# Strip one's first product by sets, three of them at two levels, in an attention and MLP kernel

## The chip, the cores and the metric

The kernel runs on one core of a Trainium2 chip, as one launch. Its time is the device time of one execution in microseconds (us). The engines of the core work side by side: TensorE (PE) multiplies matrices, VectorE (DVE) and GpSimd (POOL) do elementwise work, ScalarE (ACT) copies and applies functions, and SyncE (SP) issues the transfers between DRAM and the on-chip memory (SBUF). Products come out in banks of a second memory, PSUM, which DVE and ACT read.

## The reference

Linear attention with a normalisation, then an MLP with a squared ReLU, all in float32. q, k and v have the shape (8, 8, 576, 64), w_in is 512 x 2048 and w_out 2048 x 512.

```
kv = einsum('bhsd,bhse->bhde', k, v)
out = einsum('bhsd,bhde->bhse', q, kv)
rms = sqrt(mean(out * out, axis=-1, keepdims=True) + 1e-06)
x = (out / rms * g_norm).transpose(0, 2, 1, 3).reshape(4608, 512)
r = maximum(x @ w_in, 0.0)
result = (r * r) @ w_out
```

## The kernel before

The 4608 tokens are cut into nine strips of 512, a strip into four tiles of 128. Each strip has a first product (x times w_in, then ReLU and square) and a second product (times w_out). PE is saved work by Strassen's scheme in Winograd's form: a product of 2 x 2 blocks is done as seven products of sums of the blocks, and sums of these seven give the four quarters of the result. At one level a product has seven sets; at two levels each set is itself done as seven small products.

- Strip 0's first product is done plainly, its second at one level.
- Strip 1 (`DEEP` = 1) has its first product at one level (`up`, L889) and its second at two (`down_deep`). `up` goes through four groups g of the columns of w_in, and in each through the seven sets p of `ORDER`. Each of the 28 steps is eight matmul instructions of 128 x 256 in the trace. The banks are called A, B and C; `combine` (L845) lets ACT copy the banks of sets 1, 6 and 5 into snapshots (L849), DVE adds a later bank to a snapshot (L902) and does ReLU and square in one instruction (L903), and ACT does both for the last quarter (L907, L908).
- Strips 2 and on (`DEEP_UP` = 2) have both products at two levels. Their first product runs over 55 slots (`up_slot`): the set number n of `UP_SETS` = (1, 6, 7, 5, 2, 3, 4) has its small products (`up_small`) in slots 7n, 7n+2, up to 7n+12. Small products come out in banks A, B and C too: j = 1, 6, 5 are copied or added to snapshots (ACT L1300 or DVE L1295), the others added to a snapshot on DVE (L1295) into `gt`, the quarters of the result. For four sets ReLU and square on ACT (L1233, L1234) are due some slots later. `add_s1` lets POOL add quarter 22 to quarter 12, piece by piece; strip 1 does this on DVE in one instruction of 2048 elements per partition (L1149).
- The operands of the small products: `leaf_x` makes sums of x on POOL, `deep_sums_in` makes sums of blocks of w_in on POOL (seven times three instructions, L1189 and L289) during strip 1 and stores them to DRAM (`w_in_deep`, L1196), from where they are streamed for each strip; `deep_differences_in` replaces a block of w_in by a difference, on POOL, seven times, in strip 2.
- The second product streams two blocks of weights for each of its seven sets (`w_blk`, from `w_out` or `w_deep`, issued by `stream`). Its operands, sums g_s of the quarters, are made on DVE (L1038, L289); `small_products` L1066 multiplies.

The attention of later batches is cut into slices (`transposed_query` L384 on DVE, `key_value` L432 on PE, `query_means` L468 on PE, a normalisation on DVE L498 to L563) which `attend` places between the steps of a strip. A tile of x has to be turned for the first product. Batch one's last tile (n = 8, the first of strip 2's) does it in `features` with four PE transposes (L636) and a copy on ACT (L637). All later tiles go `squares_x` (a DVE transpose of small squares, L643), `send_x` (a store of 256 KB to DRAM, L652) and `fetch_x` (four fetches of 64 KB, L659).

All transfers around the change are issued by SP, in program order. At most eight are on the way: an issue waits for the landing of an older one, and for whoever writes its source or still reads its target. `clock[0]` counts planned microseconds; `tiles_due` and `keys_due` hold transfers with a due time, `drip` issues the rest in between. Blocks of weights and the w_in sums share six buffers (tag `w_blk` of `stream_pool`), the sums of x and g_s eight (`sum_pool`), and from strip 1 on the products have five banks (`fpsum`).

Of the kernel before, what the change touches and what calls it, by code (L numbers as in the profile page):

```python
# [10 lines left out]
FP32 = mybir.dt.float32  # L11
# [9 lines left out]
def kernel(  # L21
# [628 lines left out]
    def send_x(n):  # L650
        d = sent[n] = dram.tile([P, 4, NP, SQ], FP32, name="x_d", tag="x_d", bufs=2 * NT)
        nc.sync.dma_start(out=d, in_=squared.pop(n))  # L652
        tiles_due.append((clock[0] + {9: 30, 10: 36, 11: 24}.get(n, 6), fetch_x, (n,)))

# [51 lines left out]
    slices += [(query_means, (last,)), (K, (2, 0, 1)), (T, (2, 0)), (roots_normalized, (last,)), (T, (2, 1))]  # L706
    slices += [(T, (2, 2)), (T, (2, 3)), (features, (last[0],)), (K, (2, 2, 3))]
    pair_ends = []
# [179 lines left out]

    def up(s, g, p):  # L889
        open_bank(p)  # L890
        rhs = {
            1: halves(s, 0, 0), 2: halves(s, 1, 0), 3: halves(s, 1, 1),
            4: xc[s][3], 5: xc[s][0], 6: xc[s][1], 7: xc[s][2],
        }[p]
        for i in range(2):
            product(p, i, lambda kc: w_in[:, kc, g, A_IN[p], ts(i, P)], lambda kc: rhs[:, :, kc, :], KH)
        dest = quarters(s, g)

        def relu_squared(q):
            def f(b, a):  # L900
                o = dest[q]
                nc.vector.tensor_tensor(out=o, in0=b, in1=a, op=ALU.add)  # L902
                nc.vector.scalar_tensor_tensor(out=o, in0=o, scalar=0.0, in1=o, op0=ALU.max, op1=ALU.mult)  # L903
            return f

        def last(b):
            nc.scalar.activation(dest[21], b, AF.Relu)  # L907
            nc.scalar.activation(dest[21], dest[21], AF.Square)  # L908

        combine(p, relu_squared(11), relu_squared(12), last, relu_squared(22))  # L910

# [190 lines left out]
    def down_deep(s, k, i):  # L1102
        p = DEEP_ORDER[k]
        if k == i == 0:
            stream()
        if s == N_STRIP - 1 and k == 6 and i == 1:
# [19 lines left out]
            return  # L1126
        if k == 0 and s >= DEEP_UP:
            if i == 0:
                return
            for j in (7, 5, 6, 3):  # L1130
                small_products(s, p, (j,))
            stream(2)
            deque(leaf_next[1], 0)
            for slot in sorted(relus):
                relu_squares(slot)
            for slot in sorted(first_s):
                add_s1(s, slot)
            return
# [8 lines left out]
        if i == 1:  # L1147
            if k == 0:
                nc.vector.tensor_tensor(out=q12, in0=q12, in1=q22, op=ALU.add)  # L1149
            if k == 3:  # L1150
                minus(nc.vector, q22, q22, q11)
            if k == 4:
                minus(nc.vector, q21, q21, q11)
            if k == 6:
                deque(together(s, p), 0)
            return
# [22 lines left out]
    w_half = lambda b, kc, f: w_in[:, kc, 2 * f : 2 * f + 2, b]  # L1179

    def deep_sums_in(b):

        if b == 0:
            t = [sum_pool.tile([P, FQ // 2, P], FP32, name=f"w_i{i}", tag="sum") for i in range(3)]
        else:
            whole = stream_pool.tile([P, 4, FQ // 2, P], FP32, name="w_i", tag="w_blk")
            t = [whole[:, i] for i in range(3)]
        s1, s2, s4 = (x.rearrange("p f e -> p (f e)").rearrange("p (g e) -> p g e", g=2) for x in t)
        nc.gpsimd.tensor_tensor(out=s1, in0=w_half(b, 0, 1), in1=w_half(b, 1, 1), op=ALU.add)  # L1189
# [51 lines left out]
    def up_slot(s, slot):  # L1241

        for n, p in enumerate(UP_SETS):
            i, odd = divmod(slot - 7 * n, 2)
            if not odd and 0 <= i < 7:
                up_small(s, n, p, ORDER[i], slot)
# [3 lines left out]
        if at == 0 and 0 < n < 6:  # L1250
            leaf_x(s, n + 1)
        if s == DEEP_UP and at == 0 and n < 7:
            deep_differences_in(A_IN[UP_SETS[n]])
# [79 lines left out]
    for s in range(N_STRIP):  # L1333
# [11 lines left out]
        else:  # L1345
            steps = [(1, up, (s, g, p)) for g in range(NG) for p in ORDER]
        n_up = len(steps)
# [11 lines left out]
        for i, (w, fn, a) in enumerate(steps):  # L1359
# [33 lines left out]
            if s:  # L1393
                clock[0] += 3.2 if i >= n_up else 2.2 if s == DEEP else 1.2
                soon = tiles_due and tiles_due[0][2][0] // NT == s + 1
# [4 lines left out]
                elif not due(keys_due) and not (soon and due(tiles_due)):  # L1400
                    least = 2.1 if s == DEEP else 4.5 if i < n_up else 3.3
                    quiet = n_up * 2 // 3 < i < n_up + 3 or s == DEEP and i > n_up + 9
                    quiet = quiet or s == DEEP and i < n_up and drips and drips[0][0] == load_q_rest
# [3 lines left out]
                if s == DEEP:  # L1407
                    attend(begun + (goal - begun) * min(i + 1, 25) // 25)
                elif i < n_up:
                    attend_between(i, begun, goal, *(2, 34) if s == DEEP_UP else (0, 27), 38)  # L1410
                if s == DEEP and i in (3, 4, 7, 9):
                    if i == 3:
                        last_sums = store_deep_sums(*deep_due.popleft())
                    next(last_sums, None)
                if s == DEEP and i == n_up - 3:
                    leaf_sums(s, 4)
                if s == 1 and i in range(2, 23, 3):
                    deep_sums_in((1, 6, 5, 4, 0, 2, 3)[i // 3])
                if s == 1 and i in (17, 20, 21, 23):
                    stream()  # L1420
# [59 lines left out]
```

## Time and profile before

| | |
|---|---|
| median of 7 runs | 887.17 us (886.42 to 889.76) |
| profiled execution | 886.42 us, a span of 884.6 us in the trace |
| strip 1's first product | 138.6 to 195.4 us of the span |
| strip 1's second product | 195.4 to about 237 us |
| strip 2's first product, with the first set of its second | about 237 to 295 us |
| granted clock of PE | 1.00 in all of these |

Two rows of its transfers with large blocks are `w_blk` from `w_deep`, 1024 KB and 7.1 us from issue to landing (median of 56), and `w_blk` from `w_in_deep`, 768 KB and 5.5 us (of 49).

How to read the profile: times are us from the start of the span. "busy" is the time in which an engine executed something. A group row gives the line, the engine, the operation, the output and inputs, the shape and the count, then the busy time and the mean duration in ns, and then the idle time of the engine just before it with who ended it. A timeline row begins with start and duration. Matmuls overlap their neighbours a little, so the distance of two starts is what one costs. SPq is the queue of issues on SP.

### The profile page before, as it was taken

To read this page: it belongs to the slowest core of one execution; us is meant where nothing else is said; L and a number is where in the kernel's file an instruction comes from. 1 tells how busy PE (TensorE), PEld (TensorE's weight loads), DVE (VectorE), ACT (ScalarE), POOL (GpSimd) and SP (SyncE) were. 2 spreads that over 40 slices of the span, in tenths; PEclk is the share of its full clock that TensorE was granted. 3 is DMA by queue.
4 is the path that set the end of the run, shared out by engine and by line. 5 is a ranking of instruction groups with operands and counts; after the bars stand their busy time and mean duration, and the time that the engine had idled before them with its cause. 6 is when DMAs were issued, how large, how long until landed. Compare 5 with 4: busy or idle time off the path is not lost.

```text
span 884.6 us, 20899 instructions
## 1 busy us (share of the span) xinstructions
PE 875.8 (99%) x8296; PEld 821.5 (93%) x8296; DVE 721.6 (82%) x1239; ACT 352.4 (40%) x805; POOL 307.9 (35%) x316
## 2 busy tenths in 40 slices
PE   8999999999999999999999999999999999999998
PEld 7445888889999999999999999999999999999998
DVE  4999998879778985798778966897888778866887
ACT  4898242320049203740365034902491147102710
POOL 0000005610549133731474045604570447045700
PEclk9999999999999999999999999999999999999999
DMA  9998998999979997889678978897668665884483
GB/s 316 312 315 249 296 380 240 270 349 336 310 197 262 328 330 221 223 323 316 209 216 296 321 226 237 294 335 228 207 218 302 255 211 184 291 295 163 175 314 108
DMA packets 170257, 235.73 MB, mean 266 GB/s; under 512 B 79536, under 2 KB 134576, under 8 KB 161840
## 3 DMA queue, kind: packets, MB, share of 16 engines
q1 hardware_dynamic: 169856, 234.33, 80.8%
q8 instruction: 65, 1.06, 0.5%
q14 instruction: 32, 0.26, 0.1%
q10 hardware_dynamic: 304, 0.07, 0.0%
HBM read 197.66 MB, written 36.70 MB: 265 GB/s over the span
## 4 chain that ended last, share of the span: by engine, by line
PE 94%; ACT 2%; DMA 1%; DVE 1%; SPq 0%; issue 0%; DVEq 0%
PE ps_B L1066 22%; PE ps_A L1283 19%; PE ps_A L1066 17%; PE ps_B L1283 9%; PE ps_A L839 6%; PE ps_C L1283 5%; PE ps_B L839 3%; PE kv_ps L432 2%; PE ps_A L880 2%; PE x_ps L468 2%; PE ps_C L839 2%; PE ps_C L880 2%; PE ps_B L880 1%; DMA w_blk<-w_deep 1%; DMA q<-in_q_dram 1%; PE ps_A L617 1%
## 5 line engine op out<-in xcount | busy, mean ns | idle before, releaser
L1066 PE MATMUL ps_B<-w_blk,g_s 128*128 128x128 f32 x1008 | 123.9, 275 | 0.0
L1066 PEld LDWEIGHTS ps_B<-w_blk,g_s 128*128 128x128 f32 x1008 | 118.1, 192 | 0.1
L1283 PE MATMUL ps_A<-x_l,w_in 128*128 128x128 f32 x784 | 103.8, 275 | 0.3 <-ACT snap L1300 0.3
L289 POOL TENSOR_TENSOR x_l<-xT 128x256 f32<-128x256 f32 x21 | 15.7, 749 | 237.4 <-PE ps_A L1066 188.5
L1283 PEld LDWEIGHTS ps_A<-x_l,w_in 128*128 128x128 f32 x784 | 95.4, 192 | 0.6 <-ACT snap L1300 0.5
L1066 PE MATMUL ps_B<-w_blk,gt 128*128 128x128 f32 x752 | 95.4, 275 | 0.4 <-DMA w_blk<-w_deep 0.4
L1066 PE MATMUL ps_A<-w_blk,g_s 128*128 128x128 f32 x768 | 93.6, 275 | 0.0
L1066 PEld LDWEIGHTS ps_B<-w_blk,gt 128*128 128x128 f32 x752 | 89.6, 192 | 0.7 <-PE ps_B L1283 0.6
L1066 PEld LDWEIGHTS ps_A<-w_blk,g_s 128*128 128x128 f32 x768 | 89.6, 192 | 0.0
L1295 POOL TENSOR_TENSOR snap<-snap,gt 128x512 f32<-128x512 f32 x35 | 45.9, 1311 | 118.7 <-ACT snap L1300 104.4
L1300 ACT COPY snap<-ps_A 128x512 f32<-128x512 f32 x63 | 37.0, 587 | 109.6 <-PE ps_A L1283 100.9
L1233 ACT ACTIVATE gt<-gt 128x512 f32<-128x512 f32 x112 | 70.1, 626 | 12.8 <-DVE gt L1295 12.7
L1066 PE MATMUL ps_A<-w_blk,gt 128*128 128x128 f32 x576 | 72.2, 275 | 0.0
L1234 ACT ACTIVATE gt<-gt 128x512 f32<-128x512 f32 x112 | 70.6, 631 | 3.6
L1066 PEld LDWEIGHTS ps_A<-w_blk,gt 128*128 128x128 f32 x576 | 68.2, 192 | 0.0
L1082 ACT COPY o_sb<-ps_A 128x128 f32<-128x128 f32 x24 | 6.4, 266 | 148.4 <-PE ps_A L1066 142.4
L1081 DVE TENSOR_TENSOR o_sb<-o_sb,ps_B 128x256 f32<-128x256 f32 (+1 forms) x123 | 47.4, 385 | 17.2 <-ACT o_sb L1082 12.3
L289 DVE TENSOR_TENSOR gt<-gt 128x2048 f32<-128x2048 f32 (+1 forms) x29 | 59.7, 2063 | 0.0
L1295 POOL TENSOR_TENSOR gt<-gt,snap 128x512 f32<-128x512 f32 x42 | 52.4, 1275 | 17.6 <-DVE snap L1295 17.4
L1283 PE MATMUL ps_B<-x_l,w_blk 128*128 128x128 f32 x392 | 52.1, 276 | 0.0
L1283 PE MATMUL ps_A<-x_l,w_blk 128*128 128x128 f32 x392 | 51.9, 275 | 0.0
L1081 DVE TENSOR_TENSOR o_sb<-o_sb,ps_A 128x256 f32<-128x256 f32 (+1 forms) x96 | 37.1, 387 | 15.1 <-ACT o_sb L1082 10.6
(193 smaller groups left out, 1819.6 us busy)
## 6 DMA issues: line engine op xcount, KB each, us to landing
w_blk<-w_deep SPq DMA_DIRECT2D x56, 1024.0 KB, 7.1
w_blk<-w_out SPq DMA_DIRECT2D x56, 768.0 KB, 6.2
w_blk<-w_in_deep SPq DMA_DIRECT2D x49, 768.0 KB, 5.5
raw<-in_moe_w_in_dram SPq DMA_DIRECT2D x16, 512.0 KB, 6.9
raw<-in_moe_w_out_dram SPq DMA_DIRECT2D x16, 512.0 KB, 5.9
k<-in_k_dram SPq DMA_DIRECT2D x29, 256.0 KB, 4.5
v<-in_v_dram SPq DMA_DIRECT2D x29, 256.0 KB, 5.2
x_d<-x_q SPq DMA_DIRECT2D x27, 256.0 KB, 5.1
```

The lines of the kernel that those rows point to most:

```text
L289: eng.tensor_tensor(out=out, in0=a, in1=b, op=ALU.subtract)
L432: nc.tensor.matmul(ps[ts(h, D), i], lhsT=a, rhs=w, start=i == 0 and c == 0, stop=c == C, skip_group_check=True)
L468: nc.tensor.matmul(ps[half, r, i, ts(p, D)], lhsT=q[row, half], rhs=kvd[b, p][row, row], start=True, stop=True)
L839: nc.tensor.matmul(bank[BANK[p]][:, i, :], lhsT=lhsT(k), rhs=rhs(k), start=p in (1, 5, 2) and i == 0 and k == 0, stop=k == n - 1, skip_gro ...
L880: nc.tensor.matmul(ps, lhsT=w_in[:, kc % KH, g, kc // KH * 2 + fh, ts(i, P)], rhs=xt[0][:, :, kc, :], start=kc == 0, stop=kc == NP - 1,)
L1066: nc.tensor.matmul(chain[c][x][:, i, :], lhsT=a[:, f, :], rhs=w[:, f, :], start=x not in opened[c] and f == 0, stop=f == FQ // 2 - 1, skip ...
L1081: add = lambda out, a, b: nc.vector.tensor_tensor(out=out, in0=a, in1=b, op=ALU.add)
L1233: nc.scalar.activation(o, o, AF.Relu)
L1234: nc.scalar.activation(o, o, AF.Square)
L1283: nc.tensor.matmul(ps[:, i, :], lhsT=w, rhs=rhs, start=j in (1, 2, 5) and i == 0, stop=True, skip_group_check=True)
L1295: add = lambda eng, out, a, b: eng.tensor_tensor(out=out, in0=a, in1=b, op=ALU.add)
L1300: nc.scalar.copy(t, ps)
```

## The change

Strip 1's first product goes set by set instead of group by group. Sets 1, 6, 7 and 5 stay at one level (`up_set`): 16 steps, each with a bank of its own, which ACT copies into the result (set 1) or DVE adds to a quarter (sets 6, 7 and 5; set 5's bank is added to two). Sets 2, 3 and 4 go through `up_slot` as in later strips, slots 28 to 54, with 21 small products. The first of these slots stand between the last steps of set 5. The second product's first set has its small products partly in slots 49, 51 and 53, as later strips have, and POOL's `add_s1` does what L1149 did.

For that POOL makes the w_in sums of sets 2, 3 and 4 first, and these stay in SBUF for strip 1 besides going to DRAM; the sums of x for these sets and three of the seven differences of w_in move from strip 2 into strip 1.

Batch one's last tile is transposed on DVE, stored and fetched like the later ones. Streams, drips and slices of attention are placed by new step numbers.

```diff
--- before.py
+++ after.py
@@ -650,7 +650,7 @@
     def send_x(n):
         d = sent[n] = dram.tile([P, 4, NP, SQ], FP32, name="x_d", tag="x_d", bufs=2 * NT)
         nc.sync.dma_start(out=d, in_=squared.pop(n))
-        tiles_due.append((clock[0] + {9: 30, 10: 36, 11: 24}.get(n, 6), fetch_x, (n,)))
+        tiles_due.append((clock[0] + {8: 50, 9: 30, 10: 36, 11: 24}.get(n, 6), fetch_x, (n,)))
 
     def fetch_x(n):
         s, i = divmod(n, NT)
@@ -704,7 +704,7 @@
     ready[1] = len(slices)
     T, K, last = transposed_query, key_value, query_pairs(1)[2]
     slices += [(query_means, (last,)), (K, (2, 0, 1)), (T, (2, 0)), (roots_normalized, (last,)), (T, (2, 1))]
-    slices += [(T, (2, 2)), (T, (2, 3)), (features, (last[0],)), (K, (2, 2, 3))]
+    slices += [(T, (2, 2)), (squares_x, last), (T, (2, 3)), (send_x, last), (K, (2, 2, 3))]
     pair_ends = []
     for b in range(2, B):
         pairs = query_pairs(b)
@@ -886,28 +886,26 @@
         for th in range(2):
             nc.scalar.activation(dest[(11, 12, 21, 22)[2 * fh + th]][:, i, :], ps[:, ts(th, TH)], AF.Square)
 
-    def up(s, g, p):
-        open_bank(p)
-        rhs = {
-            1: halves(s, 0, 0), 2: halves(s, 1, 0), 3: halves(s, 1, 1),
-            4: xc[s][3], 5: xc[s][0], 6: xc[s][1], 7: xc[s][2],
-        }[p]
+    def up_set(s, g, p):
+        rhs = {1: lambda: halves(s, 0, 0), 5: lambda: xc[s][0], 6: lambda: xc[s][1], 7: lambda: xc[s][2]}[p]()
+        ps = fpsum.tile([P, 2, TH], FP32, name="ps_D", tag="f")
         for i in range(2):
-            product(p, i, lambda kc: w_in[:, kc, g, A_IN[p], ts(i, P)], lambda kc: rhs[:, :, kc, :], KH)
+            for kc in range(KH):
+                nc.tensor.matmul(
+                    ps[:, i, :], lhsT=w_in[:, kc, g, A_IN[p], ts(i, P)], rhs=rhs[:, :, kc, :],
+                    start=i == kc == 0, stop=kc == KH - 1, skip_group_check=True,
+                )
         dest = quarters(s, g)
-
-        def relu_squared(q):
-            def f(b, a):
-                o = dest[q]
-                nc.vector.tensor_tensor(out=o, in0=b, in1=a, op=ALU.add)
-                nc.vector.scalar_tensor_tensor(out=o, in0=o, scalar=0.0, in1=o, op0=ALU.max, op1=ALU.mult)
-            return f
-
-        def last(b):
-            nc.scalar.activation(dest[21], b, AF.Relu)
-            nc.scalar.activation(dest[21], dest[21], AF.Square)
-
-        combine(p, relu_squared(11), relu_squared(12), last, relu_squared(22))
+        add = lambda q, a: nc.vector.tensor_tensor(out=dest[q], in0=ps, in1=dest[a], op=ALU.add)
+        if p == 1:
+            nc.scalar.copy(dest[11], ps)
+        elif p == 5:
+            add(22, 21)
+            add(12, 12)
+            nc.scalar.activation(dest[22], dest[22], AF.Relu)
+            nc.scalar.activation(dest[22], dest[22], AF.Square)
+        else:
+            add(*{6: (12, 11), 7: (21, 12)}[p])
 
     for p, t in zip((1, 2, 5), w_first):
         w_blk[0, p] = t.rearrange("p f (h e) -> p h f e", h=2)
@@ -1101,7 +1099,7 @@
 
     def down_deep(s, k, i):
         p = DEEP_ORDER[k]
-        if k == i == 0:
+        if k == i == 0 and s >= DEEP_UP:
             stream()
         if s == N_STRIP - 1 and k == 6 and i == 1:
 
@@ -1124,7 +1122,7 @@
                         eng = nc.scalar if j == 3 else nc.sync
                         send_quarter(s, 0, 1, o, *divmod(to.start, 2), eng)
             return
-        if k == 0 and s >= DEEP_UP:
+        if k == 0:
             if i == 0:
                 return
             for j in (7, 5, 6, 3):
@@ -1145,8 +1143,6 @@
             stream()
         q11, q12, q21, q22 = (gq[s, q] for q in (11, 12, 21, 22))
         if i == 1:
-            if k == 0:
-                nc.vector.tensor_tensor(out=q12, in0=q12, in1=q22, op=ALU.add)
             if k == 3:
                 minus(nc.vector, q22, q22, q11)
             if k == 4:
@@ -1178,6 +1174,8 @@
 
     w_half = lambda b, kc, f: w_in[:, kc, 2 * f : 2 * f + 2, b]
 
+    IN_SET = {b: p for p, b in A_IN.items()}
+
     def deep_sums_in(b):
 
         if b == 0:
@@ -1185,6 +1183,8 @@
         else:
             whole = stream_pool.tile([P, 4, FQ // 2, P], FP32, name="w_i", tag="w_blk")
             t = [whole[:, i] for i in range(3)]
+            if UP_SETS[4:].count(IN_SET[b]):
+                w_blk["in", DEEP, IN_SET[b]] = whole.rearrange("p n f e -> p n (f e)")
         s1, s2, s4 = (x.rearrange("p f e -> p (f e)").rearrange("p (g e) -> p g e", g=2) for x in t)
         nc.gpsimd.tensor_tensor(out=s1, in0=w_half(b, 0, 1), in1=w_half(b, 1, 1), op=ALU.add)
         minus(nc.gpsimd, s2, s1, w_half(b, 0, 0))
@@ -1242,14 +1242,14 @@
 
         for n, p in enumerate(UP_SETS):
             i, odd = divmod(slot - 7 * n, 2)
-            if not odd and 0 <= i < 7:
+            if not odd and 0 <= i < 7 and (s > DEEP or n >= 4):
                 up_small(s, n, p, ORDER[i], slot)
         if slot in SUM_AT:
             sum_x(s, SUM_AT[slot])
         n, at = divmod(slot, 7)
         if at == 0 and 0 < n < 6:
             leaf_x(s, n + 1)
-        if s == DEEP_UP and at == 0 and n < 7:
+        if at == 0 and n < 7 and (s == DEEP_UP and n < 4 or s == DEEP and n > 4):
             deep_differences_in(A_IN[UP_SETS[n]])
         relu_squares(slot)
         add_s1(s, slot)
@@ -1343,7 +1343,14 @@
         elif s == 0:
             steps = [(2, up_first, (g, fh, i)) for g in range(NG) for fh in range(2) for i in range(2)]
         else:
-            steps = [(1, up, (s, g, p)) for g in range(NG) for p in ORDER]
+            x_sums[s, 4] = xc[s][3]
+            by_set = [(2, up_set, (s, g, p)) for p in UP_SETS[:4] for g in range(NG)]
+            small_ones = [(1, up_slot, (s, slot)) for slot in range(28, 55)]
+            steps = by_set[:13] + small_ones[:1] + by_set[13:14] + small_ones[1:3] + by_set[14:15]
+            steps += small_ones[3:5] + by_set[15:] + small_ones[5:]
+            small_steps = {28, 30, 32, 34, *range(35, 55)}
+            work = [2 if fn == up_set else a[1] in small_steps for _, fn, a in steps]
+            passed = [sum(work[: i + 1]) / 2 for i in range(len(steps))]
         n_up = len(steps)
         if s < DEEP:
 
@@ -1391,7 +1398,7 @@
                 convert(3 + i)
             done += w
             if s:
-                clock[0] += 3.2 if i >= n_up else 2.2 if s == DEEP else 1.2
+                clock[0] += 3.2 if i >= n_up else 1.1 * work[i] if s == DEEP else 1.2
                 soon = tiles_due and tiles_due[0][2][0] // NT == s + 1
                 if i == n_up + 10:
                     while tiles_due and tiles_due[0][2][0] // NT == s + 1:
@@ -1399,24 +1406,27 @@
                         f(*a)
                 elif not due(keys_due) and not (soon and due(tiles_due)):
                     least = 2.1 if s == DEEP else 4.5 if i < n_up else 3.3
-                    quiet = n_up * 2 // 3 < i < n_up + 3 or s == DEEP and i > n_up + 9
+                    quiet = s > DEEP and n_up * 2 // 3 < i < n_up + 3
+                    quiet = quiet or s == DEEP and (i > n_up + 9 or i < n_up + 3 and passed[min(i, n_up - 1)] > 19)
                     quiet = quiet or s == DEEP and i < n_up and drips and drips[0][0] == load_q_rest
                     if not quiet and clock[0] >= dripped[0] + least:
                         dripped[0] = clock[0]
                         drip(True)
                 if s == DEEP:
-                    attend(begun + (goal - begun) * min(i + 1, 25) // 25)
+                    attend(begun + (goal - begun) * min(int(passed[min(i, n_up - 1)]), 23) // 23)
                 elif i < n_up:
                     attend_between(i, begun, goal, *(2, 34) if s == DEEP_UP else (0, 27), 38)
                 if s == DEEP and i in (3, 4, 7, 9):
                     if i == 3:
                         last_sums = store_deep_sums(*deep_due.popleft())
                     next(last_sums, None)
-                if s == DEEP and i == n_up - 3:
-                    leaf_sums(s, 4)
-                if s == 1 and i in range(2, 23, 3):
-                    deep_sums_in((1, 6, 5, 4, 0, 2, 3)[i // 3])
-                if s == 1 and i in (17, 20, 21, 23):
+                if s == DEEP and i in (1, 3, 5, 7, 10, 12, 15):
+                    deep_sums_in({1: 6, 3: 2, 5: 3, 7: 1, 10: 5, 12: 4, 15: 0}[i])
+                if s == DEEP and i == 8:
+                    leaf_x(s, 4)
+                if s == DEEP and i == 9:
+                    deep_differences_in(2)
+                if s == DEEP and i in (18, 22):
                     stream()
                 continue
             if i == n_up:
```

## The prediction

> **What bounds the kernel now.** I read the page's busy times and its chain of waits first:
>
> ```profile
> PE 875.8 (99%) x8296; PEld 821.5 (93%) x8296; DVE 721.6 (82%) x1239; ACT 352.4 (40%) x805; POOL 307.9 (35%) x316
> ...
> PE 94%; ACT 2%; DMA 1%; DVE 1%; SPq 0%; issue 0%; DVEq 0%
> ```
>
> TensorE (PE) is the whole story: 875.8 of 884.6 us busy, 94% of the chain. Its work has to shrink, or something has to make it wait. An average can hide a stage, so next I took the busy times of four stretches: strip 1's first product (138.2 to 195.4), its second product, and strip 2's first product in two parts.
>
> ```profile
> core 0: us, PE busy (x) PEld busy (x) DVE busy (x) ACT busy (x) POOL busy (x), PEclk, DMA share, GB/s
> ...
> 138.20:195.40 57.20, 57.20 (x512) 49.37 (x512) 45.96 (x71) 16.54 (x34) 29.60 (x21) 1.00 0.94 281
> 195.40:237.00 41.60, 41.60 (x375) 41.60 (x374) 39.27 (x59) 2.82 (x8) 7.08 (x7) 1.00 0.98 323
> 237.00:287.00 50.00, 50.00 (x607) 49.25 (x606) 36.44 (x63) 30.77 (x79) 36.06 (x38) 1.00 0.87 242
> 287.00:333.00 46.00, 45.28 (x403) 44.93 (x402) 39.75 (x61) 7.35 (x16) 12.51 (x13) 1.00 0.94 331
> ```
>
> PE never pauses before 287. But VectorE (DVE) has only 11.24 us to spare in strip 1's first product, and the DMA share is 0.94 to 0.98. So a gain on PE is limited by DVE and DMA, not by ScalarE (ACT) or GpSimd (POOL). The clock is 1.00, so no gain or loss comes from there.
>
> **The change part by part.** *Products.* The timeline of PE, start, length, line and shape, once in strip 1 and once in strip 2:
>
> ```profile
> 191.80 1.89 PE L839 MATMUL ps_B<-xT,w_in 128*128 128x256 f32 x8
> 193.53 1.89 PE L839 MATMUL ps_A<-x_t,w_in 128*128 128x256 f32 x8
> ...
> 276.71 1.06 PE L1283 MATMUL ps_A<-x_l,w_blk 128*128 128x128 f32 x8
> 277.61 1.06 PE L1283 MATMUL ps_A<-x_l,w_in 128*128 128x128 f32 x8
> ```
>
> Starts, not lengths, give the price, because neighbours overlap: a large product costs 193.53-191.80 = 1.73 us (1.726 over several), a small one 277.61-276.71 = 0.90 (0.893 over several). Before, strip 1 has 28 large products: 48.33 us. After, it has 16 large ones (four sets, four groups) and 21 small ones (three sets): 27.62 + 18.75 = 46.37. That is -1.96 us. The small products of the second product's first set only move into the first product: same number, same price.
>
> *The last tile of batch one.* Its four PE transposes go; four such took 0.44 us on PE. -0.44 us. In their place DVE does one transpose (0.70, the same form that later tiles use), and SP issues one store of 256 KB and four fetches of 64 KB. 512 KB at the 302 GB/s moved between 210 and 236 us is 1.7 us of DMA time, on no engine's path as long as the weight blocks keep their lead; the third rival prices the case where they don't. The store waits for its DVE transpose and holds the loads queued behind it on SP.
>
> So PE alone gains 2.40 us. All else can only take from that, except in strip 2.
>
> *DVE.* Added: 16 adds of a bank (L899 of the new file) and 18 adds of the small products at 0.68, one transpose at 0.70: 23.8 us. Removed: 12 adds L902 at 0.68, 12 relu-and-multiply L903 at the 1.01 of the row below, and L1149 of 2.29 us: 22.6 us. The total hardly moves (+1.2 us), but its place does: the early adds wait for nobody, while from slot 32 on PE needs each sum to get a bank back.
>
> ```profile
> L903 DVE SCALAR_TENSOR_TENSOR gt<-gt 128x512 f32<-128x512 f32 x12 | 12.1, 1010 | 0.4
> ...
> 161.46 0.71 DVE L384 STREAM_TRANSPOSE qT<-q 128x512 f32<-128x512 f32 x1 [2.38 <-DMA q<-in_q_dram]
> ```
>
> *First place, slot 32.* The second row is a transpose that waits for its q: DVE lay idle 2.38 us, until 161.46. In the new order the sums of the fifth large set stand behind that same wait. If q lands when it did, DVE is free at 162.1 and then has about 11 us to do before the sum that slot 32 waits for: two sums of weights (0.65 and up to 1.3), six bank adds (0.62 apart: 3.7), two reductions (1.27), the mean, the root and its Newton steps (1.2), two scalings (1.29), one more transpose (0.70) and the sum itself (0.68): 173.0. Counting PE's products and attention work from 138.6 by the prices above, PE gets there at 171.7. Between 0 (q lands 1.3 us sooner) and 1.3 us; I take 0.4, because the wait before is that of one late transfer and the queue ahead of it changes.
>
> *Second place, slots 35 to 54.* These are the very slots of strip 2, so strip 2 shows what they cost PE:
>
> ```profile
> PE ps_B L1066 <- DMA w_blk<-w_deep: 0.4, 1, 0.4
> PE ps_B L1283 <- DVE snap L1295: 0.3, 1, 0.3
> ...
> 194.30 0.69 DVE L289 TENSOR_TENSOR g_s<-g_s,gt 128x512 f32<-128x512 f32 x1
> ...
> 280.20 1.11 DVE L1038 TENSOR_TENSOR g_s<-gt 128x512 f32<-128x512 f32 x1
> 282.43 1.80 DVE L289 TENSOR_TENSOR g_s<-g_s,gt 128x512 f32<-128x512 f32 x1
> ...
> 282.41 1.27 POOL L289 TENSOR_TENSOR w_in<-w_in 128x512 f32<-128x512 f32 x1
> ```
>
> The first two rows are all that PE waited for between 195 and 300 us: 0.3 us for a DVE sum in these slots. The rows below tell why it is so near: a sum g_s of two SBUF tiles takes 0.69 us with POOL idle (194.30) and 1.11 to 1.80 with POOL at work (282.43, beside POOL's 282.41). Before, strip 1 makes its g_s with POOL idle; after, POOL adds there and differences w_in there as well. Strip 1 also carries about 2 us of the second batch's attention in these slots, which strip 2 doesn't. By counts DVE has 16.1 to 18.5 us to do for 16.1 us of PE, so the cost is 0 to 2.4 us; I take the row of the same slots, 0.3.
>
> The Trainium skill, "SBUF — State Buffer", "Who interferes with whom", calls the port pair that VectorE and GpSimd share an exclusive lock: with two SBUF inputs VectorE is blocked for the whole GpSimd instruction. It speaks for the new bank adds, which read one SBUF input, and against the g_s sums here: blocked for a whole 1.27 each, five of them would take 9.8 us, and slots 35 to 54 would cost some 6 us; the 1.11 to 1.20 of most rows says that a part of the block is usually over when DVE comes.
>
> *Strip 2* loses three of POOL's differences of w_in, two of them (277.70 and 282.41) amid the g_s above. The 0.3 us wait should go with them: -0.3 us (0 to -0.3). The wait of 0.4 us for a weight block stays.
>
> *POOL* gets three differences, three sums of snaps and four additions at 1.27 and three operand sums at 1.74 into 138 to 195 us: 17.9 us on top of 29.60, of 55. It hides in the idle 25 us. Its additions end last, and DVE's next reader of them comes only in the third set of the second product.
>
> *ACT* gets some 40 instructions and loses 21, about 0.6 us each, on 16.54 of 57.2: hidden.
>
> **Sum.** -1.96 - 0.44 + 0.4 + 0.3 - 0.3 = -2.0 us. The profiled run took 886.42 (a span of 884.6 and 1.8 around it) and would take 884.4. The median of the runs is 887.17, 0.75 above it; from there it is 885.2 us.
>
> **The rivals.** *DVE takes the saving.* Both places at their upper ends, 1.3 + 2.4, and no relief in strip 2: -2.40 + 3.7 = +1.3, 888.5; at the middle of both, 0.65 + 1.2, -0.55, 886.6. For it: DVE is at 80% of the stage and moved to its end, with 2 us of attention. Against it: strip 2 does the same slots for 0.3. As the likely time of this case I take 887.2: no change.
>
> *Late transfers decide, slower.* The place is the run of weight blocks that strip 1's second product reads. SP issued the two blocks of its sixth product late:
>
> ```profile
> 224.23 0.45 SPq L937 DMA_DIRECT2D w_blk<-w_out x1
> ...
> 226.28 0.38 SPq L943 DMA_DIRECT2D w_blk<-w_deep x1
> ...
> w_blk<-w_deep SPq DMA_DIRECT2D x3, 1024.0 KB, 7.4
> ```
>
> The first lands, at the 7.4 us of the neighbouring blocks, at 231.6, and PE's sixth product starts at 232.77: a lead of 1.1 us. The new order ends the strip 2 us sooner, puts a fourth tile's fetches (four, about 0.39 us of SP each: 1.6) and 1.7 us of DMA time before these blocks, and POOL's sums, stored in another order, can hold SP while PE or DVE is late. It decides once more than about 1.1 us of delay reach these blocks. 2 + 1.6 + 1.7 - 1.1 = 4.2 us of waiting against 2.4 gained: +1.8, 889.0, and more if the first blocks (issued from 180 on) slip too. Against it: the extra fetches may be issued before the queue is tight, and an earlier free buffer lets blocks start sooner.
>
> *Nothing held up at all*: both places 0, -2.7, 884.5; inside the forecast's own range.
>
> **Numbers.** A measurement of this kernel tells about 0.2%, 1.8 us, from no change. Forecast, faster: 0.46; DVE takes the saving, no change: 0.27; late transfers or a worse DVE, slower: 0.27. The time is the forecast's, 885.2; its own range 884.3 to 886.2. The whole range takes in no hold-up at the low end, with the median's 0.5 us of scatter (884.0), and at the other end most of the slow case, 889.6. Faster 0.46, same 0.27, slower 0.27.
>
> **What would show it.** Strip 1's first product should end at about 193 to 194 us by PE's own work (moved small products left out), with the second product of it free of waits. PE's waits should list a DVE sum around slot 32 and one or two in the slots after 35, under 1 us together; over 2 us there is the first rival. Waits of L1064 for w_blk over 0.5 us between 190 and 237 are the second. g_s in strip 1 should take 1.1 to 1.2 us instead of 0.69; strip 2's 0.3 us wait should be gone. The prediction is wrong if q lands later than 161.5, if POOL's sums make PE wait, or if strip 2 waits where it didn't.

## The result, and the profile after

The changed kernel is slower: 890.88 us (median of 19 runs, 889.09 to 897.9) against 887.49 (46 runs of the kernel before); the ratio is 1.0039, with a 95% interval of 1.0029 to 1.0050, some 3.4 us. The forecast was 885.2. The profiled execution took 890.58 us, a span of 888.8, which is 4.2 us longer than the span before.

The page's busy times and chain, as shown of the kernel before:

```profile
PE 876.0 (99%) x8364; PEld 823.1 (93%) x8364; DVE 720.6 (81%) x1249; ACT 362.8 (41%) x823; POOL 320.8 (36%) x332
...
PE 80%; DVE 9%; DMA 7%; ACT 2%; issue 1%; SPq 1%; DVEq 0%; ACTq 0%
```

PE is no less busy than before (875.8), although its work shrank, and its share of the chain fell from 94% to 80%: DVE and DMA now hold it up. PE's own waits between 100 and 300 us say where (who waited, for whom, us in total, times, the longest):

```profile
PE kv_ps L432 <- DMA v<-in_v_dram: 2.5, 1, 2.5
PE ps_B L1283 <- DVE snap L1295: 1.4, 2, 1.3
PE ps_A L1283 <- DVE snap L1295: 0.3, 1, 0.3
PE ps_A L839 <- DVE o_sb L1009: 0.3, 1, 0.3
PE ps_B L1064 <- DMA w_blk<-w_deep: 0.2, 1, 0.2
```

And PE's timeline around the first two (start, length, line, what; in brackets the idle time before and who ended it):

```profile
175.21 1.05 PE L1283 MATMUL ps_B<-x_l,w_i 128*128 128x128 f32 x8
176.20 0.69 PE L432 MATMUL kv_ps<-v,k 128*64 128x64 f32 x16
179.42 1.12 PE L432 MATMUL kv_ps<-v,k 128*64 128x64 f32 x16 [2.54 <-DMA v<-in_v_dram]
...
181.03 1.80 PE L468 MATMUL x_ps<-kv_all,qT 64*64 64x64 f32 x60
...
198.22 1.06 PE L1064 MATMUL ps_B<-w_blk,gt 128*128 128x128 f32 x8
200.54 1.16 PE L1283 MATMUL ps_B<-x_t,w_i 128*128 128x128 f32 x8 [1.26 <-DVE snap L1295]
```

Three things are to be read here. The key-value product stops halfway for a v that is not there, 2.54 us. The matmuls after it are slow: 16 of them take 1.12 us, where the same 16 took 0.69 just before, and 60 products of x take 1.80 instead of 1.10. And at slot 52 PE waits 1.26 us for a sum on DVE. The window from 176 to 184 shows the slow ones in the granted clock, 0.79:

```profile
core 0: us, PE busy (x) PEld busy (x) DVE busy (x) ACT busy (x) POOL busy (x), PEclk, DMA share, GB/s
176.00:184.00 8.00, 5.38 (x118) 4.92 (x117) 2.38 (x5) 5.63 (x11) 7.33 (x8) 0.79 1.08 303
197.00:207.00 10.00, 8.74 (x78) 8.55 (x77) 9.06 (x12) 6.72 (x12) 5.69 (x4) 1.00 0.82 316
```

The balance of strip 1, from its first product to the first large group of its second product's second set: 138.45 to 201.50 before, 63.05 us; 138.92 to 206.89 after, 67.97. If PE's work there shrank by the 2.4 that the prediction priced, some 7.3 us were lost. By distances of starts: 2.7 for v, 1.5 for slow matmuls, 1.4 at slot 52, 1.0 in slots 45 to 47, 0.5 at slot 32, the rest in pieces of 0.1. Strip 1 began 0.5 us later, and some 1 us came back after it.

Why v is late is seen on SP's timeline. After, and then before:

```profile
170.15 0.68 SPq L132 DMA_DIRECT2D k<-in_k_dram  x1
170.88 0.63 SPq L132 DMA_DIRECT2D v<-in_v_dram  x1
171.60 0.50 SPq L1196 DMA_DIRECT2D w_in_deep<-w_i  x1
172.19 0.38 SPq L132 DMA_DIRECT2D k<-in_k_dram  x1
172.63 1.36 SPq L132 DMA_DIRECT2D v<-in_v_dram  x1
```

```profile
166.77 0.42 SPq L132 DMA_DIRECT2D k<-in_k_dram  x1
167.24 0.50 SPq L132 DMA_DIRECT2D v<-in_v_dram  x1
167.83 0.42 SPq L132 DMA_DIRECT2D k<-in_k_dram  x1
168.30 0.47 SPq L132 DMA_DIRECT2D v<-in_v_dram  x1
```

The second v goes out at 172.63 instead of 168.30. Counted on SP's timelines from 138 us on, 1.9 MB more than before stand ahead of it: two more stores of w_in sums (768 KB each, one of them between the two pairs), one more store of a turned tile (256 KB) and two more pieces of q (64 KB each). At the 296 GB/s moved from 160 to 176 us that would be some 6.6 us (an estimate). This v also took 6.7 us to land instead of 5.4, so it was there about 5.6 us later than before. Over the whole span the changed kernel moves only 0.55 MB more (236.28 against 235.73): most of the 1.9 MB is the same transfers in another order.

### The profile page after: what moved, and what is told of

The parts are those of the page before. It is cut to its first block, busy times and chain, and to the rows that moved or that the text cites. A ratio compares the mean times of both kernels' runs of the same rounds, so it can differ in the third digit from the quotient of the medians.

```text
span 888.8 us, 21096 instructions
## 1 busy us (share of the span) xinstructions
PE 876.0 (99%) x8364; PEld 823.1 (93%) x8364; DVE 720.6 (81%) x1249; ACT 362.8 (41%) x823; POOL 320.8 (36%) x332
## 2 busy tenths in 40 slices
DMA packets 170979, 236.28 MB, mean 266 GB/s; under 512 B 79616, under 2 KB 135168, under 8 KB 162560
## 4 chain that ended last, share of the span: by engine, by line
PE 80%; DVE 9%; DMA 7%; ACT 2%; issue 1%; SPq 1%; DVEq 0%; ACTq 0%
PE ps_B L1064 22%; PE ps_A L1283 19%; PE ps_A L1064 17%; PE ps_B L1283 9%; PE ps_C L1283 5%; PE ps_D L894 3%; DMA v<-in_v_dram 2%; PE kv_ps L432 2%; PE x_ps L468 2%; DVE w_c L269 2%; DVE w_t L289 1%; DMA q<-in_q_dram 1%; DMA w_deep<-w_t 1%; DVE wt L289 1%; DMA raw<-in_moe_w_in_dram 1%
## 5 line engine op out<-in xcount | busy, mean ns | idle before, releaser
L1283 PE MATMUL ps_A<-x_l,w_in 128*128 128x128 f32 x832 | 110.2, 275 | 0.3 <-ACT snap L1300 0.3
L1283 PEld LDWEIGHTS ps_A<-x_l,w_in 128*128 128x128 f32 x832 | 101.2, 192 | 0.8 <-ACT snap L1300 0.5
L1295 POOL TENSOR_TENSOR snap<-snap,gt 128x512 f32<-128x512 f32 x38 | 49.7, 1309 | 130.2 <-ACT snap L1300 112.1
L1233 ACT ACTIVATE gt<-gt 128x512 f32<-128x512 f32 x124 | 77.6, 626 | 17.6 <-DVE gt L1295 17.4
L1234 ACT ACTIVATE gt<-gt 128x512 f32<-128x512 f32 x124 | 78.2, 631 | 3.9
L1173 POOL TENSOR_TENSOR gt<-gt 128x512 f32<-128x512 f32 x32 | 52.8, 1670 | 0.0
```

Source lines behind the costliest of these rows:

```text
L1173: nc.gpsimd.tensor_tensor(out=a, in0=a, in1=b, op=ALU.add)
L1233: nc.scalar.activation(o, o, AF.Relu)
L1234: nc.scalar.activation(o, o, AF.Square)
L1283: nc.tensor.matmul(ps[:, i, :], lhsT=w, rhs=rhs, start=j in (1, 2, 5) and i == 0, stop=True, skip_group_check=True)
L1295: add = lambda eng, out, a, b: eng.tensor_tensor(out=out, in0=a, in1=b, op=ALU.add)
```

## The experiments

Each was timed beside runs of the kernel before on the same chip; "before" is their median.

### Is it the place of a few transfers in the queue?

The stores of the w_deep parts and one store of w_in sums behind the loads of k and v:

```diff
             for _ in deep_sums(parts, w):
                 if p == 4:
                     yield
+            if p == 4:
+                yield
             for i, t in enumerate(parts):
                 nc.sync.dma_start(out=w_deep[B_OUT[p], :, i], in_=t)
...
-                if s == DEEP and i in (3, 4, 7, 9):
+                if s == DEEP and i in (3, 4, 7, 9, 14):
```

> The changed kernel, but in strip 1 the four stores of w_deep parts and one store of w_in sums are issued behind the loads of k, v and their rests instead of ahead of and between them. Theory A (the late v is the loss): these loads go out some 3 us sooner, PE's pause of 2.54 us for v goes and with it the slow matmuls after it, about 1.4 us; 890.9 - 3.9 = about 887, the waits for DVE sums staying at about 1.3 us at slot 52. Rival B (DVE is the bound and the pause only hides it): the wait for v goes, but the waits for DVE sums grow by as much; within 1 us of the changed kernel, 890 to 891.

Measured: 894.46 us, before 886.97; 1.0078 (1.0059 to 1.0096). The wait for v did go, and yet it is slower than the changed kernel. PE's timeline and two windows of it:

```profile
184.88 1.06 PE L1288 MATMUL ps_A<-x_t,w_in 128*128 128x128 f32 x8
191.99 2.04 PE L1288 MATMUL ps_A<-x_l,w_in 128*128 128x128 f32 x8 [6.05 <-ACT snap L1305]
193.83 1.91 PE L1288 MATMUL ps_C<-x_t,w_in 128*128 128x128 f32 x8
```

```profile
184.00:192.00 8.00, 1.95 (x19) 1.78 (x17) 3.78 (x7) 0.85 (x3) 6.62 (x8) 0.92 0.60 193
192.00:197.00 5.00, 5.00 (x23) 5.00 (x24) 4.90 (x11) 3.46 (x7) 4.15 (x3) 0.50 1.02 402
```

The wait is put down to a copy on ACT, but ACT had 0.85 of 8 us to do. POOL is what stood: busy 0.68 us from 176 to 184, where it had 7.33, very likely because its next sums share their eight buffers with the w_deep parts, whose stores were now issued from 176.3 to 179.3 (the trace itself names PE as what released it); it caught up in the window shown (6.62). Neither theory foresaw that. The second window shows something else: after 6 us of pause the clock is 0.50 and a small product takes 1.91 us instead of 1.06.

One q behind k and v, and nothing else moved:

```diff
+                    quiet = quiet or s == DEEP and 8 <= i < 13
                     if not quiet and clock[0] >= dripped[0] + least:
```

> The changed kernel, but the four loads of one q, which DVE needs only at 185.5 us, are issued behind the loads of k and v that PE needs at 176, not ahead of them; the stores stay where they are. Theory A (the queue ahead of v is the loss): k and v go out about 2 to 3 us sooner, the wait for v is under 0.5 us, the granted clock is 1.00 in nearly all runs, and the time falls by 2.5 us and the share of slow matmuls (1 us on average): 887 to 888, about the kernel before. Rival B (DVE is the bound, the pause only hides it): waits for DVE sums grow from 1.5 to 3 or more, 889.5 or above.

Measured: 889.95, before 887.23; 1.0026 (1.0012 to 1.0040). The wait for v fell to 0.5 us, but PE's and DVE's timelines have a new pair:

```profile
195.74 1.98 PE L1283 MATMUL ps_A<-x_l,w_in 128*128 128x128 f32 x8 [2.06 <-DVE gt L1295]
```

```profile
194.40 0.71 DVE L643 STREAM_TRANSPOSE x_q<-x_n 128x512 f32<-128x512 f32 x1 [1.93 <-DMA x_d<-x_q]
```

DVE waits 1.93 us for the store of an earlier turned tile, whose buffer it is to write, and PE waits at slot 47 for the sum behind that transpose. Behind this pause the matmuls are slow again (1.98 us instead of 1.06). The number is the one that the rival gave, the mechanism is not: DVE was idle, and waited for a transfer.

So the tile stores were taken off SP's queue and issued by ACT:

```diff
-        nc.sync.dma_start(out=d, in_=squared.pop(n))
+        (nc.scalar if 8 <= n <= 12 else nc.sync).dma_start(out=d, in_=squared.pop(n))
```

> The changed kernel, with the stores of five turned tiles (8 to 12) issued by ACT instead of SP; everything else in SP's order stays. Theory C (what is lost is the place in one queue of transfers that is always full: whichever load is moved ahead, another comes late): one store less stands ahead of v, so the wait for v shrinks from 2.5 to about 1.5 to 2 us and the clock drops in fewer runs; 889.5 to 890.3. Theory A in its first form (the order of v alone): the same, since v's own order is unchanged but for one transfer.

> Both: q behind k and v, and the five stores issued by ACT. In the kernel with q behind k and v alone, the wait for v was replaced by one of 2.1 us for DVE, which itself stood still 1.93 us for the store of a turned tile (its buffer is written again). With that store off SP's queue, both waits should be gone: theory C gives PE waits in strip 1 of about 1.5 us in all and 887 to 888. If DVE's own work is the bound, the waits for DVE sums stay at 3 us or more: 889.5.

> The same and the quarter sum on DVE instead of POOL's four additions: a further 0.3 to 0.6 us less, 886.5 to 887.5, level with the kernel before or slightly faster.

Measured: 899.74, 894.24 and 895.77, before 888.16; ratios 1.0130, 1.0075 and 1.0075. All three missed. SP's waits in the first of them:

```profile
SPq L132 <- DMA x_d<-x_q: 6.1, 1, 6.1
```

SP's load of v shares no data with the tile store, but its turn came at 173.7 and it went out at 179.87, when the store that ACT had issued at 176.15 had landed. In the trace both use the same completion semaphore. When ACT issued its next store, at 179.00, only two other transfers were on the way, so it was not the number in flight that held the load: it seems that eight slots are given out in program order over both queues, and that this load had the slot of that store. A second queue gave no second lane; PE's wait for v grew to 5.8 us.

### Or the amount of transfers?

The stores of three w_in sums, which nobody reads in DRAM before strip 2, some 20 us later; then with the quarter sum on DVE; then with a fourth store:

```diff
-        nc.sync.dma_start(
+        put = lambda: nc.sync.dma_start(
...
+        if b in (2, 6, 3):
+            puts[b] = put
+        else:
+            put()
...
+                if s == DEEP and i in (16, 20, 24,):
+                    puts.pop({16: 2, 20: 6, 24: 3}[i])()
```

> The changed kernel, with the DRAM stores of the w_in sums of sets 2, 3 and 4 (768 KB each; strip 1 uses them from SBUF, DRAM is read only from strip 2 on) issued in steps 16, 20 and 24 instead of 1, 3 and 5. Theory C (the number of transfers ahead of v in one full queue): q, k and v land some 2.5 us sooner, the wait for v falls below 0.3, no clock drop, DVE's sums at slot 32 come in time; what stays are the 1.3 to 1.5 us of waits for DVE sums in slots 46 to 52: 887 to 888, level with the kernel before. If only the total amount of transfers in strip 1 counts, the stores now delay the tile stores or the first weight blocks, and a new wait of 1.5 to 2.5 us stands there: 889.5 to 891.

> The same, and quarter 12 += quarter 22 on DVE at the end of the set instead of four additions on POOL: another -0.3 to -0.6 us, 886.5 to 887.5.

> As the last, with the store of set 5's... fourth w_in sum, which stands between the two pairs of k and v loads, issued after them as well: the same as the last within 0.5 us if v is already in time, up to 1 us less if it is not.

Measured: 890.73, 891.2 and 890.19, before 887.96; 1.0040, 1.0040 and 1.0032 (1.0018 to 1.0046). The second branch came true. v is in time in all three, and in the last the clock is 1.000 in all nine runs; but there PE waits 1.1 us at slot 47 for a DVE that waits for a tile store, and 1.5 us in strip 2, at 269.76, for a DVE that waited 6.18 us for a q. In the first of them PE waits 1.3 us at slot 47 and 0.5 us for a weight block. In these three, moving transfers only moved the wait.

Then the three stores were left out altogether:

```diff
-        nc.sync.dma_start(
+        if b not in (2, 6, 3):
+          nc.sync.dma_start(
...
-                nc.sync.dma_start(out=w_blk[u][:, 0:3], in_=w_in_deep[A_IN[p]].rearrange(...))
+                nc.sync.dma_start(out=w_blk[u][:, 0:3], in_=w_in_deep[A_IN[5 if p in (2, 3, 4) else p]].rearrange(...))
```

> The changed kernel without the DRAM stores of the w_in sums of sets 2, 3 and 4 (later strips read set 5's in their place): 2.25 MB less in strip 1, nothing moved. If the sum of transfers is the bound, the wait for v and the clock drops go and no wait for a transfer, or for a DVE that waits for one, takes their place in strip 1 or 2; what stays are DVE's own waits in slots 32 to 52 (1.5 to 2.7 us): 887 to 888.3. If the order alone is at fault, a new wait of over 1 us for a transfer appears and the time is 889.5 or more, as when the stores were issued later.

Measured: 887.5, before 887.67; 1.0005 (0.9990 to 1.0020). All that PE waited for after 60 us:

```profile
PE ps_B L1284 <- DVE snap L1296: 1.4, 2, 1.3
PE ps_A L1284 <- DVE snap L1296: 1.2, 1, 1.2
PE ps_A L839 <- DVE o_sb L1009: 0.5, 1, 0.5
PE ps_B L1064 <- DMA w_blk<-w_deep: 0.4, 1, 0.4
PE ps_A L1284 <- ACT snap L1301: 0.3, 1, 0.3
PE ps_B L1064 <- DMA w_blk<-w_out: 0.2, 1, 0.2
```

With 2.25 MB less nothing takes the place of the wait for v, and the clock is 1.000 in 11 of 12 runs. What is left are mainly DVE's sums: 1.2 us at slot 32 and 1.4 in slots 45 to 52. The bytes and the number of transfers fall together here, so the run does not tell which of them counts.

### What makes DVE late?

The quarter sum on DVE instead of POOL's four additions:

```diff
-            if p == 3:
+            if p == 3 and s > DEEP:
                 first_s.setdefault(slot + 3, []).append(u)
...
+            if s == DEEP:
+                q12, q22 = gq[s, 12], gq[s, 22]
+                nc.vector.tensor_tensor(out=q12, in0=q12, in1=q22, op=ALU.add)
```

> The changed kernel, but strip 1's quarter 12 += quarter 22 is done by DVE in one 2048-wide instruction at the end of its first set, as in the kernel before, instead of four additions on POOL. If POOL's additions slow DVE's sums g_s (1.15 to 1.38 us instead of 0.68) and so cause the wait at slot 52, the g_s around 197 to 203 us take 0.68 and that wait of 1.26 us falls below 0.5; DVE gets 2.3 us more in the second product, where it has 1.9 of 30 us idle: -0.5 to -1 us in all. If the second batch's attention on DVE causes the wait, it stays above 1 us, and the time is the same or up to 1 us longer.

Measured: 890.22, before 886.97; 1.0032 (1.0018 to 1.0045), not told apart from the changed kernel's 1.0039. DVE's timeline in the changed kernel, and in this one:

```profile
196.81 1.38 DVE L289 TENSOR_TENSOR g_s<-gt,g_s 128x512 f32<-128x512 f32 x1
...
198.71 1.17 DVE L289 TENSOR_TENSOR g_s<-gt 128x512 f32<-128x512 f32 x1
```

```profile
195.57 1.39 DVE L289 TENSOR_TENSOR g_s<-gt,g_s 128x512 f32<-128x512 f32 x1
...
197.48 0.68 DVE L289 TENSOR_TENSOR g_s<-gt 128x512 f32<-128x512 f32 x1
```

POOL's additions are what makes the later g_s slow (1.17 against 0.68), but the one ahead of them is slow in both, and the wait at slot 52 fell only from 1.26 to 0.77. Contention is a part, about 0.5 us. (These rows bear on the Trainium skill, "SBUF — State Buffer", "Who interferes with whom", whose exclusive lock would let such a sum wait out a whole addition of POOL. POOL's three additions beside these rows took 1.70 us each; 1.17 - 0.68 = 0.49 us is what the sum lost here.)

Two of the g_s sums later, with q behind k and v, and the three edits together:

```diff
-        if slot in (41, 43, 45, 47):
+        if slot in ((41, 43, 50, 52) if s == DEEP else (41, 43, 45, 47)):
             next(leaf_next[4])
-        if slot in (49, 51):
+        if slot in (49, 51) and s > DEEP:
```

> The kernel with q behind k and v, and in strip 1 two of the g_s sums of the second product's first set made in slots 50 and 52 instead of 45 and 47, and those of its second set made after slot 54 instead of in slots 49 and 51. If it is the amount of DVE's work ahead of the bank sums in slots 45 to 52 that makes PE wait, whoever slows it, the wait of 1.26 us at slot 52 goes (under 0.3): 1 to 1.3 us less than with q behind k and v alone, 886 to 887. If it is not, the same.

> That kernel, and quarter 12 += quarter 22 on DVE at the end of the set instead of on POOL in slots 44 to 54. If POOL's additions are what slows DVE there: a further -0.4 to -0.8 us, waits for DVE sums around 1 us in all, 886.3 to 887.3. Otherwise the same as without.

> All three edits. PE's saving of 2.4 us with waits in strip 1 of some 0.7 us in all: 885.5 to 886.5, faster than the kernel before (about 887.2) by about 1 us. If it is not below 887, something else eats the saving, and the place will be seen in PE's waits.

Measured: 890.56 (1.0034, 1.0018 to 1.0051), 889.59 (1.0021, 1.0009 to 1.0034) for q and the quarter sum alone, and 890.77 (1.0037), before 887.23. With the g_s later the wait at slot 52 is gone, but that shows nothing of the g_s: with q behind k and v alone it is gone too, where PE had paused 2.06 us at slot 47 and DVE had caught up. The waits that come from transfers are not gone: 1.3 us at slot 47 and 2.1 us for a block of w_out in strip 2 in the first, 2.1 us at slot 47 and 1.0 for a block of w_out with all three edits.

At last four DVE transposes of the second batch's attention were left out, in the changed kernel, in the one with four stores later, and in the one with three stores less:

```diff
         t = x_n.pop(n)
+        if 9 <= n <= 12:
+            squared[n] = t.rearrange("p (f q d) -> p f q d", f=4, q=NP)
+            return
```

> The changed kernel without the DVE transposes of tiles 9 to 12 (x of these tiles goes to DRAM unturned): four instructions, 2.8 us less on DVE, all in strip 1; the transfers are the same. If DVE's own work is the cause of the waits in slots 46 to 52 (1.5 us), these fall below 0.3, while the wait for v of 2.5 us and the clock drops stay: 889.3 to 889.8, 1.3 less than the changed kernel. If DVE is held by something else, the same as the changed kernel.

> The kernel with four stores of w_in sums issued later and the quarter sum on DVE, without the same four transposes. With v in time and 2.8 us less on DVE, both causes are out of the way: waits in strip 1 below 1.5 us in all, 886.5 to 888. If it stays at 889.5 or more, there is a third cause.

> The same, and tiles 9 to 12 go to DRAM unturned (four DVE transposes less). Both causes out of the way: PE's saving of 2.4 us shows, less about 1 us at slot 32: 885.7 to 887, below the kernel before on the same chip by 0.5 to 1.7 us.

Measured: 889.24 against 887.4 before, 1.0017 (1.0004 to 1.0030); 891.26 against 887.4, 1.0039; and 886.56 against 887.67, 0.9987 (0.9975 to 0.9999). PE's waits in the first:

```profile
PE kv_ps L432 <- DMA v<-in_v_dram: 2.7, 1, 2.7
PE ps_A L1286 <- DVE snap L1298: 0.7, 1, 0.7
...
PE ps_B L1286 <- DVE snap L1298: 0.2, 1, 0.2
```

2.8 us less on DVE took the wait at slot 52 away, 1.6 us of time, with v as late as ever. The second missed: PE waits 2.55 us at 250, behind a DVE that waited 5.89 us for a q, and 0.9 for a block of w_out, transfers again. The third is the only kernel below the one before, and it leaves out both transfers and work on DVE. The stretch of strip 1 that took 63.05 us before takes 62.83 in it (139.33 to 202.16), with 1.4 us of PE's waits inside: at least 1.6 of the 2.4 us priced are really saved. The kernel before without the same transfers and transposes was not run; PE's waits in it after 60 us are 1.0 us in all, so it should have little to gain.

### The tile part alone, and the slow matmuls

The kernel before with batch one's last tile stored and fetched like later ones:

```diff
-    slices += [(T, (2, 2)), (T, (2, 3)), (features, (last[0],)), (K, (2, 2, 3))]
+    slices += [(T, (2, 2)), (squares_x, last), (T, (2, 3)), (send_x, last), (K, (2, 2, 3))]
```

> The kernel before, with one part of the change alone: batch one's last tile transposed on DVE, stored and fetched like the later ones. By the prediction's term: four PE transposes less, -0.4 us, 887.0. Rival: its store and four fetches delay the loads behind them on SP and PE waits for k, v or a weight block: +0.5 to +2 us.

Measured: 889.2, before 886.97; 1.0022 (1.0011 to 1.0034). The number is the one that the rival gave, but its cause explains only a part. PE waited 1.8 us in strip 1 for an L902 sum and 1.0 us for a block of w_out in strip 2. DVE's timeline, and PE's, in strip 1:

```profile
149.23 0.20 DVE L496 RECIPROCAL rms<-rms 128x8 f32<-128x8 f32 x1 [2.43 <-ACT rms L491]
...
152.93 0.68 DVE L902 TENSOR_TENSOR gt<-ps_A,snap 128x512 f32<-128x512 f32 x1
...
158.60 0.66 DVE L643 STREAM_TRANSPOSE x_q<-x_n 128x512 f32<-128x512 f32 x1
```

```profile
153.67 1.99 PE L839 MATMUL ps_A<-x_t,w_in 128*128 128x256 f32 x8 [1.79 <-DVE gt L902]
```

The 1.8 us are over before the tile is transposed (158.60) and stored (164.00), so they do not come from its transfers. The list of slices is one entry longer, `attend` therefore starts them a step earlier, and DVE stands 2.43 us for a root on ACT ahead of the sum that PE needs; before, that sum (149.83) stood ahead of the root (151.73). The changed kernel has no L902 sums. Only the 1.0 us in strip 2 is a wait for a transfer, and so this run does not tell what the tile's transfers cost in the changed kernel. The opposite, the changed kernel with the old way for this tile, was not tried: strip 2's xT would hold one of the six stream buffers while three sets of w_in sums keep theirs.

PE kept busy ahead of the product that pauses:

```diff
+        if (b, ps_of[0]) == (3, 0):
+            keep_busy(ps[:, 0], 36)
         half = slice(REST * (b % 2), REST * (b % 2 + 1))
```

> The changed kernel, with 36 matmuls of 128x64 whose result is overwritten put ahead of the key-value product that pauses for v, so that PE is busy for most of the 2.54 us. If the slow matmuls after the pause (granted clock 0.79 in 176 to 184) come from the pause, they run at full speed: added work makes it faster by about 1 to 1.4 us, 889.5 to 889.9. If the low clock has another cause, the same or up to 0.3 us slower.

Measured: 895.1, before 886.97. The filling was mis-sized: it took 8.15 us (72 records), not about 2.5, so the time says little. But the wait for v is gone, and the window has a full clock where the changed kernel has 0.79:

```profile
176.00:184.00 8.00, 8.00 (x74) 8.00 (x73) 2.38 (x4) 4.04 (x7) 7.38 (x8) 1.00 1.14 313
```

All six runs of it have a mean clock of 1.000. Of the changed kernel's 20 recorded runs 7 have 1.000 (median 889.47 us), 10 have 0.998 (891.3) and 3 have 0.996 (892.84). Without the pause the clock stays, with it it drops in most runs. By these medians that goes with 1.8 us more in the ten and 3.4 in the three, 1.4 over all; how long the pause was is known for the profiled one alone.

## Why the prediction was wrong

*The products.* Right: 28 large ones became 16 large and 21 small, PE's pitch is close to the price (1.74 and 0.89 us against 1.73 and 0.89), and with most of what holds PE up taken away the kernel falls below the one before.

*Batch one's last tile.* The step set -0.44 us and left the 512 KB "on no engine's path as long as the weight blocks keep their lead". The weight blocks kept their lead, and yet the tile's store is one of the transfers ahead of the late v, 256 of 1920 KB. In the kernel before the part alone costs some +2 us, but most of PE's wait there comes from another placing of slices. Its share in the changed kernel is open.

*The missing term.* This is the step that failed most: the sum put transfers at nothing. It had two places where PE could wait, both on DVE; a load of k and v was in neither. The late-transfer rival had the cause (a longer queue, w_in sums stored in another order, PE sooner at every point) but looked for it at the sixth set's weight blocks, where PE did not wait at all. It was the load needed at 176 that came late. That place and its clock drop cost about 2.7 and 1.5 us; of the clock the text had said that "no gain or loss comes from there". The profile had shown the DMA share at 0.94 to 0.98 in these stretches, and the text named it as a limit, but left it at nothing in the sum. Seven orders of the same transfers gave 889.6 to 899.7 us, each with PE waiting somewhere for a transfer or for a DVE or POOL held up by one, and 2.25 MB less gave 887.5. So the new order needs more room for transfers than strip 1 has. The amount alone is not the cause: the kernel before moves 0.55 MB less in all and has no such wait.

*Slot 32.* 0.4 expected, 0.3 waited: right in number, but with some luck: with v in time it is 1.2, near the upper end of 1.3 given.

*Slots 35 to 54.* This term was mis-sized: 0.3 taken, 1.4 measured as PE's waits (0.19 and 1.26) and 2.4 by distances of starts, which is the upper end given. The row of strip 2 was the wrong one to take: strip 1 carries the second batch's transposes in these slots, and without four of them the wait at slot 52 is gone. The 2 us of attention stood in the text and should have moved the value.

*Strip 2.* Its wait of 0.3 us for a DVE sum is gone, as forecast; the 0.4 for a weight block, which was to stay, is 0.2.

*POOL and ACT.* As said, both hid in the changed kernel: no wait of over 0.3 us for them, ACT's 0.3 being there before. Three of POOL's four additions took 1.70 us, not 1.27, and they slowed DVE's g_s.

Still open: whether some order of the full set of transfers in strip 1, with two or three DVE instructions moved out of slots 35 to 52, would reach the forecast. None that was run did; the best complete one, q behind k and v with the quarter sum on DVE, is at 1.0021.

## What to carry to other kernels

Where the DMA share is near 1 in a stretch, a saving on the bound engine asks for every transfer sooner, and each added transfer can have a price even if its own reader has time: list what each load behind it on the queue is needed for, k and v as well as weights. Take one transfer away, not only to another place, to see whether amount or order is at fault. And a stage that serves as the model for another one must carry the same side work.

## What the runs showed of the hardware

A pause of 2 to 3 us on PE can cost more than itself. After 2.54 us the granted clock fell for some 3 us (0.79 over 176 to 184), after 6.05 us it was 0.50 for 5 us. In other traces of this case it also fell after 2.06, 2.08 and 2.14 us, but not after 2.18 and 2.61, nor after any pause of up to 1.85. The Trainium skill, "TensorE: Matmul & The Clock Gate", "Why this matters for your kernels", asks for no gaps over about 3 us; here 2.06 us was enough in one trace, and the measurement decides.

Transfers issued by two engines shared one limit: a load of v on SP waited 6.1 us for the landing of a store that ACT issued.
